# A new order for all queues of a pooled-attention and gated-convolution kernel, with ScalarE's one-column copy first

## The chip, the cores and the metric

The kernel runs on one core of a Trainium2 chip. A core has five engines, and the program gives each its own queue of instructions: TensorE (PE, with its weight loads shown apart as PEld), VectorE (DVE), ScalarE (ACT), GpSimd (POOL) and SyncE (SP). POOL and SP compute little here; they issue transfers. An engine waits on another only through semaphores. The metric is the device time of one execution in microseconds (us).

## The reference

The inputs are q, k and v, each 8 batches x 8 heads x 576 rows x 64 columns, and three weights. For each batch and head:

```
k_p, v_p = means of k and v over groups of 8 rows            # 576 -> 72 rows
attn     = softmax(q @ k_p.T / 8);  x = attn @ v_p           # heads side by side: 576 x 512
h        = relu(x @ w_in)                                    # 576 x 1024
conv     = w0 * h[row-1] + w1 * h[row] + w2 * h[row+1]       # per column of h, zero outside
out      = (h * sigmoid(conv)) @ w_out                       # 576 x 512
```

All inputs and the output are float32; the kernel computes in bf16 with float32 sums.

## The kernel before

**Attention of a batch.** k and v are added up over groups of 8 rows (three additions on DVE, or eight products with the identity on PE, `pmv`). PE transposes the sums of k (`kT`), and two copies spread them into `kz` (`kz.b.0`, `kz.b.1`). q is loaded by head and turned so that columns lie on partitions (`qT`, then the copies `qTe`); for batches 6 and 7 SP does that with transposing transfers (`qD`). A tile of scores is `sc` on PE and its exponential `exp` on ACT. Five tiles `av.b.t` per batch multiply with v; the reciprocal of the row sum and the scaling are `rc` and `nm` on DVE (lines 683 and 687). x is transposed by PE (`xt`, copied by `xte`), or from batch 3 on by SP (`xD`).

**The rest of a batch.** h comes in eight blocks of 128 columns, f = 0 to 7: `mm1.b.f` on PE and `relu.b.f` on ACT. The convolution goes by pairs of blocks, in one of three forms, which the table `alt` gives per pair ("c1.3" is the pair of blocks 2 and 3 in batch 1): form 0 works off PE, with two products by a tap (`cp0`, `cp2`, either on ACT, line 769, or on DVE, line 771), two additions on DVE (`ca0`, `ca2`, lines 776 and 781) and the sigmoid on ACT as a tanh (line 788); form 2 does both blocks on PE, with three diagonal weights per block (`dw`, line 407 on ACT or 409 on DVE, made once at the start for each block number that any pair needs) and the tanh straight from PE's result (line 805); form 1 does the first block off PE and the second on PE. Then DVE computes the gate (`tg1`, line 832) and the product (`g`, line 838). Two batches are a pair; its 9 tiles of 128 output rows are `mm2` on PE (line 863) with eight products each, a copy `oe` (ACT, line 888, or DVE) and a store.

**Batch 0** is treated apart so that work can start early: k comes in float32 through SP, q in two loads, of 64 and of 32 partitions (`ldq0.0` and `ldq0.1`, line 250). Scores, exponentials and `mm1` of batch 0 are split the same way, x = 0 for the larger part. Until data arrive, PE multiplies zeros (`fill`, line 231).

**What sets the order.** All work is first written down as 1,077 operations with their dependences. The table `order` is one list of these operations' numbers; every engine's queue is that list with the other engines' operations left out. An entry such as 77@B0 also gives the operation its PSUM buffer (three of kind A, two of kind B), and 106A0/77 puts 106 blocks of fill, of 128 columns each, ahead of it. The table `act` names the operations that may run on either engine and shall run on ACT; the rest of those run on DVE. So nothing of the order is decided at run time, and an instruction that waits holds up all that stands behind it on its engine.

**ScalarE's first operation.** `aw` copies one column of a small tile `wrm` (line 341); no other operation reads its result. ScalarE needs its function table loaded once, and the built program places that load ahead of ScalarE's first computing instruction, whichever that is.

Of the kernel before, what the change touches and what calls it, by code (L numbers as in the profile page):

```python
# [16 lines left out]
        "15 52 0 41 4 47 18 53 49 19 48 61 50 60 57 3 59 5 16 73 56 54 74 58 55 75 76 65 106A0/77@B0 6@B1 84@A0 7 36 21 78 86 17 85 62 42 "  # L17
        "17A1/80@B1 44 40 64 82@A1 81 63 79 87 83 139 88 35A2/98@B0 94@B1 43 106@A0 99 89 102@A1 140 100@A2 95 110@B0 90 103 112@B1 91 34 "
        "111 92 107 93 29 101 114@A0 23 39 108@B0 119@A1 113 115 109 124@A2 116 25 104@B1 96@B0 125 105 117@A0 97 126 118 120 13B1/129@A2 "
        "20 121 127@B0 134@A0 27 128 130 122@B1 33 156@A1 131 32 123 154@B0 135 152@A2 136 35 203@B1 155 204 8 132@A0 31 9 223@B0 28 205 51 "  # L20
        "157 133 137@B1 69 224 10 138 158 146 198@A0 153 199 201@B1 70 22 147 218@A1 200 226@A2 11 67 148 225 219 68 1 14 202 206@A0 24 227 "
        "13 149@B0 220 208 221@B1 210 150 252@A1 12 66 231 222 151 207 254@B1 26 229 253 169@A0 45 165@A2 37 209 240@B0 170 30 228 242@A1 "
        "166 232 163@A0 71 72 243 238@A2 211 164 212 143 256@A1 239 213 241 167@A0 255 244@A2 257 283 258@B0 245 171@A1 215 284 248@A2 172 "
        "285 277 259 144 46 230 286@B1 168 233 291@B0 249 289@A1 38 293@A0 214 290 246@A2 294 234 260@A1 216 235 287 217 262@A0 288 247 292 "
        "159@B1 263 250 236 261 301@A0 251 280 309@A2 160 302 141 161 307@A1 162 310 237 3B0/173@A0 281 308 305@A2 145 174 264 306 "
        "3B0/178@A1 175 3B0/183@A2 265 188@A0 142 176@B0 179 276 184 266@B1 295 180 177 401 189 185 400 190 186@B0 267 181@A1 191@A0 193@A2 "
        "187 268@B1 194 278 279 195 282 296 303@A2 192 269 271@B0 297 182 298 304 299 300 407 196@B1 272 311@A0 316@A1 197 408 321@A2 317 "
        "273@B0 409 312 322 520 318 323 521 326@A1 313 274 410@B1 419 413@A2 327 411 328 417@B0 415@A0 412 418 361@A1 416 539 375@A0 362 "
        "527 336@A1 376 528 414 351@A0 529 337 329@B0 352 431@A1 433@A2 420 432 319@B1 434 429@A0 341 349@A1 330 320 421 430 427@A2 422 "
        "314@B0 350 424 525 331@A0 366 428 324@B1 340 403 373@A1 332 405 333 406 425@A2 423 374 359@A0 342 402 325 343 355@A1 364 426 650 "  # L30
        "360 435@A2 643 530@B1 356 353@A0 531 315 363 532 338@A1 436 437 354 440@A2 339 438@B0 441 334@B1 357 344 444@A0 442 345@A1 522 439 "
        "367 537@A2 335 346 535@B0 538 533@B1 536 471@A1 380 534 365 379 445 549@A2 377 472 368 660@B0 550 656@B1 446 658@A1 369 553@A2 347 "
        "447 483@A0 659 657 378 554 651 485@A1 443 484 348 370 652 545@A0 498@A2 661 765 546 381 2 644 486 458@A0 524 382 499 404 448@A1 "
        "371 459 551@A2 523 372 653@B0 552 662 456@A0 449 384 358 496@A2 383 450 457 451 385 469@A1 654 386 655 452@A0 476 470 387@B1 453 "
        "487 454 540 497 455 461 547@A0 460 672@A1 541 270 673 670@A2 503 390@B0 542 671 462 649 543 548 647 463 473 771 645 668@A0 492@A1 "
        "669 544 646 772 555@A2 388 526 488 559@A0 493 556 489 392@B1 648 464 560 490 502 778 557 589@A1 777 558 561 474 563@A2 500 605@A0 "
        "780 773 393 501 590 564 774@B1 565 606 465@A1 779 504 775 676@A0 475 477 591@A2 466 275 505 562 391 478 567@A1 677 395@B0 568 491 "
        "467 566 569 592 663 479 389 571@A0 570 468 577@A1 776 480 572 573 674@A2 578 397@B1 664 574 506 494 665 675 495 768 507 789@A0 770 "
        "481 787@A1 616@A2 790 767 508 595 788 769 593 575@A0 781 617 782 596 603@A1 666 764 509 576 766 791@A2 667 604 618@A0 482 594 607 "
        "581 700@A1 792 580 609 597 742@A2 701 579 398 582 714@A1 583 743 619 783 698@A2 584 715 608 598 678@A0 682@A1 699 679 510@B1 623 "  # L40
        "784 396 786 585 683 680 684 620 686@A2 681 612@A0 687 586 688 712@A1 685 719 587 717 613 793@A2 621 512@B0 610 689 794 588 622 892 "
        "394 713 624 690@A0 611 795@A2 691 785 728@A1 625 796 511 886 694@A2 600 515@B1 614 692 729 705 695 887 693 696 627 726@A0 615 599 "
        "697 797@A1 716 516 740@A2 718 702 626 399 601 517@B1 798 727 703 706 733 799 704 847@A0 602 800 513 628 831@A1 848 629 514 518 "
        "801@A0 707 741 630@B0 519 730 709 802 888 708 803 720 805@A2 832 809@A0 732 806 889@B1 731 817@A1 807 890 631 893 861@A2 810 818 "
        "710 895 734 744 845@A1 746 735 894 633@B0 745 811 711 862 804 846 748 833@A0 634 721 808 891 813@A1 737 823 635@B0 896 834 747 736 "
        "837 897 722 903@A0 814 836 907@A2 638@B1 835 636 749 723 815 908 724 816 751 819@A1 738 839 904 901@A2 812 820 725 640@B0 824 821 "
        "739 632 750 637 898 905@A0 822 859@A1 849 906 825 902 909@A0 838 860 826 931@A2 851 827 866 933@A1 840 932 900 910 899 947@A2 752 "
        "934 852 828 753 911@A0 959@A1 641 865 864 948 829 754@B0 850 841 912 913 863 853 914 639 915@A0 867 945@A2 960 842 854 919@A1 935 "
        "756@B1 936 920 921 855 916 922 917 946 973@A1 856 830 642 757 937 923@A0 868 927@A2 755 759@B1 952 924 928 929 869 857 930 938 950 "
        "961@A2 925 870 843 758 975@A0 760 918 844 962 871 761@B0 976 858 926 949 872 963 939 873@B1 762 940 974 966 941 964 876@B0 980 965 "  # L50
        "967 942 874 951 1025@A0 875 978 968 763 977 1013@A1 943 970 953 1011@A2 981 1014 1026 954 1039@A1 1012 944 969 1027@A0 1016 1018 "
        "955 979 878@B1 1015 956 982 877 1017 971 1028 1019 997@A2 879 957 984 881@B0 972 983 1020 998 1029 1021 1032 999@A0 985 1003 958 "
        "883@B1 1030 986 882 1031 1033 1022 987@B0 1034 1000 884 1002 1001 1036 885 1023 989@B1 880 1004 1040 1005 1035 1006 988 1041@A0 "
        "1037 990 1038 1008 991 992@B0 1024 1007 1042 1009 1043 1010 994@B1 1045 1044 1046 993 1047 1053@A0 995 1048 996 1050 1057@B0 1049 "
        "1051 1061@B1 1052 1054 1058 1055 1062 1059 1056 1065@A0 1063 1060 1064 1066 1069@B0 1071 1070@B1 1067 1072 1068 1073 1075 1074 "
# [917 lines left out]
```

## Time and profile before

| what | value |
|---|---|
| time, median of 3 runs | 197.21 us (196.5 to 199.03) |
| profiled execution: its own time | 197.41 us |
| profiled execution: its span | 194.8 us |
| PE busy / idle in the span | 186.7 / 8.1 us |
| DVE busy | 165.9 us |
| ACT busy | 165.2 us |
| bytes read / written in HBM | 32.52 / 9.44 MB |

The span runs from the first to the last recorded instruction; the time of the same execution has 2.6 us more around it. Busy times are sums over the span, so they hide stages with different limits; matmuls overlap in the records, so a busy PE is not PE at its peak. "Idle before" an instruction is named with what ended it.

### The profile page before, as it was taken

The page shows a single profiled execution, that of the slowest core. Times are in us where ns is not written, and L with a number is a line of the kernel's source. Part 1 is how long each engine was busy: PE and PEld are TensorE (multiplying, and loading weights), DVE is VectorE, ACT ScalarE, POOL GpSimd, SP SyncE. Part 2 cuts the span into 40 slices and gives each one's busy share as a digit, 9 for nine tenths or more (in the row PEclk, how much of TensorE's full clock was granted, in tenths as well). Part 3 has the DMA queues.
Part 4 walks back from the last instruction along what each step waited for, and adds up shares of the span by engine and source line. Part 5 has one row for each costly group of instructions (what it writes and reads, how often), then busy time and mean ns, then how long its engine had stood idle before and what let it go on. Part 6 is the DMA issues. An engine that isn't in the chain of part 4 may idle for free.

```text
span 194.8 us, 4531 instructions
## 1 busy us (share of the span) xinstructions
PE 186.7 (96%) x1741; PEld 125.4 (64%) x1758; DVE 165.9 (85%) x391; ACT 165.2 (85%) x299; POOL 45.7 (23%) x85
## 2 busy tenths in 40 slices
PE   7887999999999999999999999999999999999993
PEld 2364896775687887767667766676566656655442
DVE  3563989997968799999999999999999999999720
ACT  0079999974478999999999999999999999999832
POOL 8872066086323503351044000000000000000000
PEclk9999999999999999999999999999999999999999
DMA  5999999979999997899956994659241463005344
GB/s 144 248 158 184 206 195 183 207 89 194 190 205 203 193 205 113 101 207 147 252 129 87 202 153 145 227 171 131 40 161 30 135 175 151 16 0 223 145 155 177
DMA packets 40201, 30.58 MB, mean 157 GB/s; under 512 B 18012, under 2 KB 35124, under 8 KB 40180
## 3 DMA queue, kind: packets, MB, share of 16 engines
q0 software_dynamic: 17920, 15.67, 53.0%
q1 hardware_dynamic: 22260, 14.63, 27.4%
q8 instruction: 13, 0.21, 0.5%
q14 instruction: 8, 0.07, 0.1%
HBM read 32.52 MB, written 9.44 MB: 215 GB/s over the span
## 4 chain that ended last, share of the span: by engine, by line
PE 56%; DVE 20%; ACT 16%; DMA 3%; issue 2%; DVEq 0%
PE psfB L863 20%; PE psfA L747 16%; ACT tg L788 4%; DVE xx L687 3%; PE psfA L670 3%; DMA osb<-in_k_dram 3%; DVE cv L771 3%; DVE cv L776 3%; ACT attnT L652 3%; DVE gT L838 2%; DVE cv L781 2%; PE psfA L863 2%; PE psfA L644 2%; ACT hT L738 2%; PE psfA L800 2%
## 5 line engine op out<-in xcount | busy, mean ns | idle before, releaser
L863 PE MATMUL psfB<-w_out,gT 128*128 128x512 bf16 (+1 forms) x266 | 62.1, 373 | 0.7
L747 PE MATMUL psfA<-xT,w_in 128*128 128x288 bf16 x448 | 60.6, 286 | 0.3 <-ACT hT L753 0.2
L747 PEld LDWEIGHTS <-w_in 128*128 128x128 bf16 x448 | 43.1, 98 | 14.3 <-issue 1.5
L863 PEld LDWEIGHTS <-gT 128*128 128x128 bf16 x296 | 28.5, 98 | 28.1 <-DVE gT L838 0.3
L788 ACT ACTIVATE tg<-cv,cs 128x576 bf16<-128x576 bf16 x54 | 40.9, 779 | 0.8 <-DVE cv L781 0.8
L753 ACT ACTIVATE hT<-psfA 128x576 bf16<-128x576 f32 x56 | 36.0, 658 | 2.9 <-PE psfA L747 2.6
L687 DVE TENSOR_TENSOR xx<-psfA,rr 128x512 bf16<-128x512 f32 x40 | 27.0, 684 | 0.6
L771 DVE TENSOR_SCALAR cv<-hT,cr 128x576 bf16<-128x576 bf16 x75 | 25.7, 367 | 1.1 <-ACT hT L738 0.8
L769 ACT ACTIVATE cv<-hT,cr 128x576 bf16<-128x576 bf16 x33 | 24.9, 776 | 0.1
L295 POOL DMA_DIRECT2D v_b<-in_v_dram x32 | 16.4, 517 | 36.5 <-DVE vs L533 22.9
L838 DVE TENSOR_TENSOR gT<-tg,hT 128x1152 bf16<-128x1152 bf16 x32 | 23.8, 753 | 0.2
L888 ACT COPY osb<-psfB 128x512 f32<-128x512 f32 x32 | 18.5, 588 | 5.5 <-PE psfB L863 5.5
L652 ACT ACTIVATE attnT<-psfA 128x576 bf16<-128x576 f32 x35 | 22.0, 658 | 0.1
L781 DVE TENSOR_TENSOR cv<-cv 128x1152 bf16<-128x1152 bf16 (+1 forms) x29 | 20.5, 713 | 0.5
L776 DVE TENSOR_TENSOR cv<-cv,hT 128x1152 bf16<-128x1152 bf16 (+1 forms) x29 | 20.2, 709 | 0.1
L670 PE MATMUL psfA<-vblk,attnT 128*128 128x130 bf16 x160 | 15.5, 220 | 1.3 <-ACT attnT L633 1.2
L832 DVE TENSOR_SCALAR tg<-tg 128x1152 bf16<-128x1152 bf16 x32 | 14.2, 450 | 2.6 <-ACT tg L788 2.3
L670 PEld LDWEIGHTS <-attnT 128*128 128x128 bf16 x160 | 11.9, 98 | 4.0 <-issue 1.1
L231 PE MATMUL pswA<-zero 128*128 128x512 bf16 (+1 forms) x42 | 10.9, 420 | 1.4 <-DVE zero L333 1.1
L683 DVE RECIPROCAL rr<-psfA 128x8 f32<-128x8 f32 x40 | 7.7, 199 | 4.8 <-PE psfA L674 4.8
L674 PE MATMUL psfA<-vblk,attnT 128*128 128x130 bf16 x80 | 11.2, 221 | 0.0
L644 PE MATMUL psfA<-qT,kz 128*128 128x288 bf16 x56 | 10.6, 286 | 0.0
(105 smaller groups left out, 221.2 us busy)
## 6 DMA issues: line engine op xcount, KB each, us to landing
out_dram<-osb SPq DMA_DIRECT2D x14, 512.0 KB, 3.0
q_b<-in_q_dram POOLq DMA_DIRECT2D x7, 576.0 KB, 8.1
k_b<-in_k_dram POOLq DMA_DIRECT2D x7, 512.0 KB, 9.5
v_b<-in_v_dram POOLq DMA_DIRECT2D x7, 512.0 KB, 8.6
out_dram<-osb SPq DMA_DIRECT2D x7, 256.0 KB, 2.1
osb<-in_k_dram SPq DMA_DIRECT2D x1, 1024.0 KB, 6.5
w_in<-in_moe_w_in_dram POOLq DMA_DIRECT2D x2, 512.0 KB, 10.9
w_out<-in_moe_w_out_dram POOLq DMA_DIRECT2D x2, 512.0 KB, 9.8
```

Source lines behind the costliest of these rows:

```text
L652: nc.scalar.activation(out=at(m)[:, t, :].rearrange("p (r i j) -> p r i j", i=2, j=3), in_=slot(key)[:, :, 0:HC].rearrange("p i (j r) -> p ...
L670: nc.tensor.matmul(out=a[:, g, c * w:(c + 2) * w], lhsT=attnT[m][:, S * s + u0:S * s + u0 + P], rhs=vblk[m][:, 2 * s:2 * s + 2, :].rearran ...
L687: nc.vector.tensor_tensor(out=xx[i3].rearrange("p (g h e) -> p g h e", g=2, h=4), in0=av_view()[:, :, :, 0:D], in1=rr[i3].rearrange("p (g ...
L747: nc.tensor.matmul(out=t[:, i, 0:HC], lhsT=w_in[:, c, f * P:(f + 1) * P], rhs=xT[m][:, c, i * HC:(i + 1) * HC], start=(c == 0), stop=(c == ...
L753: nc.scalar.activation(out=hT[m][:, f, 2:S + 2].rearrange("p (i x) -> p i x", i=2), in_=slot(key)[:, :, 0:HC], func=ACT.Relu)
L769: nc.scalar.activation(out=cv[y][:, kk // 2, z, :], in_=src, func=ACT.Copy, scale=sc)
L771: nc.vector.tensor_scalar(out=cv[y][:, kk // 2, z, :], in0=src, scalar1=sc, scalar2=None, op0=OP.mult)
L776: nc.vector.tensor_tensor(out=cv[y][:, 0, 0:n, :], in0=cv[y][:, 0, 0:n, :], in1=H4[:, f:f + n, 2:S + 2], op=OP.add)
L781: nc.vector.tensor_tensor(out=cv[y][:, 0, 0:n, :], in0=cv[y][:, 0, 0:n, :], in1=cv[y][:, 1, 0:n, :], op=OP.add)
L788: nc.scalar.activation(out=tg[i3][:, z, :], in_=cv[y][:, 0, z, :], func=ACT.Tanh if half else ACT.Sigmoid, scale=cs[:, f + z:f + z + 1] if ...
L838: nc.vector.tensor_tensor(out=o_, in0=tg[i3], in1=hT[b % 2][:, f:f + 2, 2:S + 2], op=OP.mult)
L863: nc.tensor.matmul(out=a[:, 0, 0:j1 - j0], lhsT=g[:, c, t * P:(t + 1) * P], rhs=w_out[:, c, j0:j1], start=(c == 0), stop=(c == n_fb - 1))
```

## The change

Only tables change; the code is the same. In `alt` one entry differs, the pair of blocks 2 and 3 of batch 1 goes from form 2 to form 1. No other pair uses block 2 on PE, so its three diagonal weights are no longer made. `order` and `act` are replaced. Fill shrinks from 180 blocks to 139; the first 106 stay.

```diff
-        "15 52 0 41 4 47 18 53 49 19 48 61 50 60 57 3 59 5 16 73 56 54 74 58 55 75 76 65 106A0/77@B0 6@B1 84@A0 7 36 21 78 86 17 85 62 42 "
...
+        "43 49 0 3 1 4 46 44 15 50 47 2 57 5 38 18 58 19 16 55 17 70 54 53 56 71 51 72 52 73 45 106A0/74@B0 6@B1 75 7 2A0/79@A0 39 83 76 8 "
...
-        "dw6.1 qTe.0.1.0 qTe.0.0.0 kz.0.1 qTe.0.0.1 dw5.2 dw2.0 dw7.1 dw2.2 xte.0.0 dw1.0 xte.0.2 dw5.0 xte.0.1 dw6.0 qTeP.1.1 dw4.2 "
...
+        "kz.0.0 kz.0.1 qTe.0.0.1 qTe.0.0.0 qTe.0.1.0 dw5.0 dw5.2 dw7.0 dw6.0 qTeP.1.1 dw7.1 dw7.2 qTeP.1.2 xte.0.1 xte.0.2 dw3.2 xte.0.3 "
...
-    "alt": {"q1": 1, "v1": 1, "c0.5": 2, "c0.7": 2, "q2": 1, "c1.1": 1, "c1.3": 2, "q3": 1, "x3.1": 1, "x3.2": 1, "x3.3": 1, "x3.4": 1, "c2.1": 1, "c2.5": 1, "q4": 1, "x4.0": 1, "x4.1": 1, "x4.2": 1, "x4.3": 1, "x4.4": 1, "c3.5": 1, "q5": 1, "x5.0": 1, "x5.1": 1, "x5.2": 1, "x5.3": 1, "x5.4": 1, "q6": 2, "x6.0": 1, "x6.1": 1, "x6.2": 1, "x6.3": 1, "x6.4": 1, "q7": 2, "x7.0": 1, "x7.1": 1, "x7.2": 1, "x7.3": 1, "x7.4": 1},
+    "alt": {"q1": 1, "v1": 1, "c0.5": 2, "c0.7": 2, "q2": 1, "c1.1": 1, "c1.3": 1, "q3": 1, "x3.1": 1, "x3.2": 1, "x3.3": 1, "x3.4": 1, "c2.1": 1, "c2.5": 1, "q4": 1, "x4.0": 1, "x4.1": 1, "x4.2": 1, "x4.3": 1, "x4.4": 1, "c3.5": 1, "q5": 1, "x5.0": 1, "x5.1": 1, "x5.2": 1, "x5.3": 1, "x5.4": 1, "q6": 2, "x6.0": 1, "x6.1": 1, "x6.2": 1, "x6.3": 1, "x6.4": 1, "q7": 2, "x7.0": 1, "x7.1": 1, "x7.2": 1, "x7.3": 1, "x7.4": 1},
```

In sums per engine: PE loses the 6 matmuls of one block's convolution. ACT gets two more tap products, one more output copy (`oe.2.4`) and one more q copy, gives up two `dw`, and has one tanh of form 0 in place of one from PE's result. DVE gets two additions for one block (half the size of a pair's), and gives up one `dw`, one output copy and one q copy; its count of tap products stays at 75.

At the head of ScalarE's queue stood the following before (dw is a diagonal weight, qT the turned q, kz the spread sums of k, attnT the exponentials, all of batch 0):

```order
L407 ACT_TABLE_LOAD
L407 ACTIVATE dw_117<-ident,cw 128x128
L573 COPY qT_87<-psbA 128x24x32
L573 COPY qT_87<-psbB 128x12x64
L507 COPY kz_85<-psbB 64x4x72
L573 COPY qT_87<-psbA 128x12x64
L633 ACTIVATE attnT_89<-psfB 128x384 x2
```

With the change the same queue begins so:

```order
L341 ACT_TABLE_LOAD
L341 COPY wrm<-wrm 128x1
L507 COPY kz_85<-psbB 64x4x72 x2
L573 COPY qT_87<-psbA 128x12x64
L573 COPY qT_87<-psbB 128x12x64
L573 COPY qT_87<-psbB 128x24x32
L633 ACTIVATE attnT_89<-psfB 128x384
```

The table load now belongs to the one-column copy, which waits only for a small memset that DVE does second; before, it belonged to a diagonal weight, which waits for the convolution's taps. Both halves of kz are now copied by ACT (DVE did one), and the larger part of q is copied first.

At the head of GpSimd's queue stood, after its constants (q_b0 takes the 64 and the 32 partitions of q, v_b0 the two halves of v and four tails of 16 partitions, all of batch 0; q_b1 and k_b1 are of batch 1):

```order
L394 MEMSET mask_65 128x780
L398 ISA
L398 AFFINE_SELECT mask_65<-mask_65 128x260 x2
L250 DMA q_b0_78<-in_q_dram 32x8x384
L250 DMA q_b0_78<-in_q_dram 64x8x384
...
L290 DMA v_b0_76<-in_v_dram 128x2x512
L282 DMA k_b1_75<-in_k_dram 64x512
L255 DMA q_b1_79<-in_q_dram 96x8x384
L398 AFFINE_SELECT mask_65<-mask_65 128x4x65
L303 DMA w_in_66<-in_moe_w_in_dram 128x4x512
```

With the change, from the same place:

```order
L394 MEMSET mask_65 128x780
L250 DMA q_b0_78<-in_q_dram 64x8x384
L398 AFFINE_SELECT mask_65<-mask_65 128x260
L250 DMA q_b0_78<-in_q_dram 32x8x384
L398 AFFINE_SELECT mask_65<-mask_65 128x260
L398 AFFINE_SELECT mask_65<-mask_65 128x4x65
L295 DMA v_b0_76<-in_v_dram 16x512
L398 AFFINE_SELECT mask_65<-mask_65 128x4x65
L295 DMA v_b0_76<-in_v_dram 16x512 x3
L290 DMA v_b0_76<-in_v_dram 128x2x512 x2
L255 DMA q_b1_79<-in_q_dram 96x8x384
L303 DMA w_in_66<-in_moe_w_in_dram 128x4x512
```

The 64-partition part of q is now the first load, the mask and all four tails stand ahead of both halves of v, and one short load of batch 1 no longer stands ahead of its q and of the first half of w_in. Not shown: three memsets and the identity now stand ahead of the mask.

Further on in the same queue (v_b0 is v of batch 2, k_b0 is k of batch 4, k_b1 k of batch 3; the 16-partition loads into v_b1 are tails of batch 3's v, which overwrite those of batch 1):

```order
L295 DMA v_b1_77<-in_v_dram 16x512
L290 DMA v_b0_76<-in_v_dram 128x4x512
L295 DMA v_b1_77<-in_v_dram 16x512
L295 DMA v_b0_76<-in_v_dram 16x512 x2
L278 DMA k_b1_75<-in_k_dram 128x4x512
```

This is what stands there with the change:

```order
L290 DMA v_b0_76<-in_v_dram 128x4x512
L282 DMA k_b1_75<-in_k_dram 64x512
L295 DMA v_b1_77<-in_v_dram 16x512 x2
L282 DMA k_b0_74<-in_k_dram 64x512
L278 DMA k_b0_74<-in_k_dram 128x4x512
L278 DMA k_b1_75<-in_k_dram 128x4x512
```

The load of batch 2's v moved ahead of the first tail of batch 3, and the load of batch 4's k ahead of that of batch 3's k.

90 rows, old and new, of the table PARAMS are left out of this document.

## Prediction

> **What bounds the kernel now.** I read the page's totals and chain first, then the busy time by stage, then the chain in order of time, and last the start by the timeline.
>
> ```profile
> span 194.8 us, 4531 instructions
> PE 56%; DVE 20%; ACT 16%; DMA 3%; issue 2%; DVEq 0%
> ```
>
> The chain of waits lies on PE for over half the span, but DVE and ACT own a third. The stages show why (columns: the stretch in us, its length, then busy us and instructions of PE, weight loads, DVE, ACT, POOL, then granted clock, DMA share, GB/s):
>
> ```profile
> 0.00:20.00 20.00, 16.61 (x183) 9.07 (x187) 9.63 (x29) 8.64 (x21) 12.88 (x29) 1.00 1.02 184
> 20.00:40.00 20.00, 19.57 (x276) 15.37 (x275) 18.26 (x53) 19.43 (x46) 7.25 (x15) 1.00 1.22 194
> 40.00:60.00 20.00, 19.77 (x229) 14.09 (x228) 16.47 (x40) 12.05 (x23) 10.02 (x16) 1.00 1.12 174
> 60.00:180.00 120.00, 119.12 (x1001) 81.05 (x1011) 116.55 (x265) 117.26 (x200) 15.52 (x26) 1.00 0.70 143
> ```
>
> From 60 to 180 us three engines are full at once: of 120 us PE idles 0.9, DVE 3.4, ACT 2.7. There an order can hardly save anything, and each new wait shows. Idle time of size stands in the first 20 us, and between 40 and 60 on ACT (8.0 us), where PE is the bound. Pieces of the chain (start, us, what) show who ends which stretch:
>
> ```profile
> 64.49 0.74 PE psfA L800 x6
> 101.13 0.65 DVE cv L771 x2
> 137.64 0.65 ACT attnT L652
> 144.93 1.14 PE psfA L747 x8
> ```
>
> The chain is on PE to about 91 us (one block's convolution, 0.74 us, lies on it), on ACT to 101, on DVE to 137, on ACT to 145, and then on PE to the end.
>
> **The start.** These are rows of the timeline (start, us, engine, line, instruction):
>
> ```profile
> 9.95 0.45 PE L501 MATMUL psbB<-ident,ksum 128*128 128x128 bf16 x5 [0.75 <-DVE ksum L482]
> 10.88 1.28 ACT L407 ACT_TABLE_LOAD   x1 [10.88 <-DVE cw L361]
> 12.17 0.40 ACT L407 ACTIVATE dw<-ident,cw 128x128 bf16<-128x128 bf16 x1
> 12.48 0.78 ACT L573 COPY qT<-psbA 128x768 bf16<-128x768 bf16 x1
> 13.99 0.39 ACT L507 COPY kz<-psbB 64x288 bf16<-64x288 bf16 x1
> 14.40 0.80 ACT L573 COPY qT<-psbA 128x768 bf16<-128x768 bf16 x1
> 15.61 0.87 ACT L633 ACTIVATE attnT<-psfB 128x384 bf16<-128x384 f32 x2 [0.41 <-PE psfB L625]
> 17.97 0.40 PE L670 MATMUL psfA<-vblk,attnT 128*128 128x130 bf16 x4 [1.16 <-ACT attnT L633]
> 18.52 0.21 DVE L683 RECIPROCAL rr<-psfA 128x8 f32<-128x8 f32 x1 [3.11 <-PE psfA L674]
> 22.86 0.83 PE L732 MATMUL psfB<-xT,w_in 128*128 128x128 bf16 x8
> ```
>
> ACT waits 10.88 us for the taps, spends 1.28 on the table load and 0.3 on the diagonal weight, and only then empties PE's buffers; the exponentials, the first `av` and all of DVE's scaling (idle 3.11) hang on that. With the change the load lies in ACT's idle time. After `kT` (9.95 + 0.45) come two kz copies of 0.39 and three q copies of 0.80: the first exponential starts at 10.4 + 0.8 + 2.4 = 13.6 in place of 15.61, and its score tile is computed under the last q copy. Ahead of the first `av` stand five wide exponentials (0.87 for two, so 0.44 each) and two narrow ones (0.35, the last row of the groups below): 13.6 + 2.9 = 16.5 in place of 17.97, a lead of **1.5 us**.
>
> Two loads must not undo it (GpSimd's queue; under the DMA rows, the last number is us from issue to landing):
>
> ```profile
> q_b<-in_q_dram POOLq DMA_DIRECT2D x1, 384.0 KB, 7.4
> v_b<-in_v_dram POOLq DMA_DIRECT2D x1, 256.0 KB, 5.6
> w_in<-in_moe_w_in_dram POOLq DMA_DIRECT2D x1, 512.0 KB, 9.1
> 7.54 0.75 POOL L290 DMA_DIRECT2D v_b<-in_v_dram  x1
> 10.84 0.80 POOL L255 DMA_DIRECT2D q_b<-in_q_dram  x1 [1.41 <-DMA q_b<-in_q_dram]
> 12.02 0.77 POOL L303 DMA_DIRECT2D w_in<-in_moe_w_in_dram  x1
> 13.26 0.56 DVE L521 TENSOR_TENSOR v_b<-v_b 128x768 bf16<-128x768 bf16 x1
> 14.95 0.29 DVE L550 TENSOR_TENSOR vblk<-vs,mask 128x256 bf16<-128x256 bf16 x1
> ```
>
> The 64-row part of q takes 7.4 us; issued at about 2.5 now, it lands by 9.9, ahead of `kT`. The 32-row part follows the mask by some 1.2 us and is needed last. The second half of v is issued about 1 us later (three tails now stand ahead), so it lands at 7.54 + 1.0 + 5.6 = 14.1; from its landing at 13.1 to the end of the last v product at 15.24 the row before took 2.1, which gives 16.2: just inside the 16.5. POOL's load of batch 1's q waited 1.41 us for a landing of batch 0's q; that wait comes earlier, and with one load less between, w_in is issued about 1 us before 12.02 and lands by some 20.1 in place of 21.1. DVE's queue then has 1.2 us of small work more between its scalings, but only 0.6 of it ahead of the tile for the first `mm1`; four reciprocals with scaling at 0.84 (18.52 to 19.37 is one) and a transposition give 17.05 + 4.0 + 0.2 = 21.3 in place of 22.86, again 1.5. Bounds: nothing, if a load is late by that much, and 2.0, the whole lead of the exponentials.
>
> **The rest of the sum.** These groups (busy us, mean ns) price the moved work:
>
> ```profile
> L800 PE MATMUL psfA<-hT,dw 128*128 128x288 bf16 x60 | 8.8, 286 | 0.0
> L788 ACT ACTIVATE tg<-cv,cs 128x576 bf16<-128x576 bf16 x54 | 40.9, 779 | 0.8 <-DVE cv L781 0.8
> L769 ACT ACTIVATE cv<-hT,cr 128x576 bf16<-128x576 bf16 x33 | 24.9, 776 | 0.1
> L805 ACT ACTIVATE tg<-psfA 128x576 bf16<-128x576 f32 x10 | 6.4, 659 | 0.1
> L888 ACT COPY osb<-psfB 128x512 f32<-128x512 f32 x32 | 18.5, 588 | 5.5 <-PE psfB L863 5.5
> L594 ACT COPY qT<-psbA 128x768 bf16<-128x768 bf16 x4 | 3.2, 811 | 0.0
> L407 ACT ACTIVATE dw<-ident,cw 128x128 bf16<-128x128 bf16 x11 | 4.5, 419 | 0.0
> L776 DVE TENSOR_TENSOR cv<-cv,hT 128x576 bf16<-128x576 bf16 x4 | 1.7, 437 | 0.0
> L633 ACT ACTIVATE attnT<-psfB 128x192 bf16<-128x192 f32 x4 | 1.1, 348 | 0.0
> ```
>
> From 20 to 40 us ACT is all but full (19.43 of 20). It has one diagonal weight less there (-0.42) and one tap product more (+0.78): +0.36. PE saves six matmuls of one convolution, **-0.74** by the chain's piece, in a stretch that PE ends; the rivals below say when that is worth nothing. The fill taken away costs and gains nothing in the sum, since the fill that went stood in waits.
>
> In the full stage ACT gets one more tap product (0.78), the output copy (0.59), the q copy (0.81) and the dearer tanh (0.779 - 0.659 = 0.12): **+2.3** against 2.7 of idle. DVE gets two half additions (0.44 each) and one tap product that went the other way at the start (0.37), and gives up the output copy (0.7 by ACT's row, the nearest) and the q copy (0.5, from the start of one 0.80 copy less DVE's faster reading, an estimate): about nothing. What ACT's extra costs is not in the trace. Below is nothing, if it all falls into ACT's idle time; above is 2.3, if none does. The chain lies on ACT for 9 + 8 of these 120 us, which is near the lower end, yet nearly all of ACT's idle would have to be used, which the order before does not do. I take a third, +0.8.
>
> The sum on the profiled execution's own 197.41 (span 194.8 and 2.6 around it): -1.5 + 0.36 - 0.74 + 0.8 = -1.1, so **196.3**. That execution was 0.2 above the median of 197.21, within the three runs' 196.5 to 199.03.
>
> By the Trainium skill's ScalarE: Activation LUTs, What ACT_TABLE_LOAD costs, a load of about 1.28 us is followed by a drain of about 1.38 us. The row of the load agrees on 1.28, but the next activation begins at 12.17, 0.01 after its end, so no drain shows here. By the page the start would gain 1.4 more and the sum would be 194.9.
>
> **The rivals.**
>
> *ScalarE takes over the bound (slower than before).* If ACT keeps its 2.7 us of waits in the full stage because its queue waits in order, its 2.3 of added work lengthens the stage in full, and PE's 0.74 is then worth nothing: 197.41 - 1.5 + 0.36 + 2.3 = 198.6, and more with every new wait. It decides once ACT uses less than 1.2 us of that idle time, which would bring back 197.4. For it: 117.26 of 120 busy. Against it: an ACT queue of more even work (tap products by batch 2 to 7 go from 5, 5, 8, 2, 8, 4 to 6, 6, 6, 6, 5, 5) where the chain was on DVE, which loses none of its slack.
>
> *The middle gains too.* Between 40 and 60 POOL's queue was held:
>
> ```profile
> 39.75 0.49 POOL L295 DMA_DIRECT2D v_b<-in_v_dram  x1 [5.31 <-PE psfA L644]
> ```
>
> That tail held batch 2's v, which now stands ahead of it. If batches 2 to 4 then start without waits, the stretch around 40 to 43, where PE did single `av` tiles between fill, gives 1.0, the start its full 2.0, and ACT's extra is hidden: 197.41 - 2.0 - 0.74 - 1.0 = 193.7. Against it: PE is the bound from 43 on, and batch 3's k now lands behind batch 4's.
>
> *The clock of PE.* The weight loads of the first fill show a clock that had to rise:
>
> ```profile
> 5.30 0.15 PEld L231 LDWEIGHTS <-zero 128*128 128x128 bf16 x1 [0.28 <-issue]
> 5.66 3.37 PEld L231 LDWEIGHTS <-zero 128*128 128x128 bf16 x16 [0.21 <-issue]
> ```
>
> Up to 5.30 one matmul took 0.43 us (0.15 and 0.28), afterwards 0.21 (3.37 by 16), though the granted clock reads 1.00 in every stage. The change takes 42 of 52 blocks of fill out of 11 to 16 us, where PE then has some 2 us of work. If it slows down again for as long as at the start (5.66 - 1.06 = 4.6 us), it loses 2.3 us: 198.6. Against it: 1.16 us without work at 17 did nothing. The Trainium skill's TensorE: Matmul & The Clock Gate, What's actually happening, has PE fall to half its clock after an idle window of about 3.4 us and rise after as long a busy one; the trace agrees with the rise, and no wait in it is long enough to show the fall. By that rule pieces of work between the waits could keep it up.
>
> *The start doesn't lead.* q or v lands over 1 us later than reckoned, and what is left of the lead is eaten by ACT: 197.41 + 0.36 - 0.74 + 0.8 - 0.3 = 197.5.
>
> **How the numbers follow.** The forecast, 195 to 197.3: 0.46. ScalarE takes over, 197.6 to 201.5: 0.24. The middle gains, 192.8 to 194.8: 0.16. The clock: 0.07. No lead: 0.07. Two per cent (193.3 to 201.2) is about what a measurement of this kernel tells from no change. Faster by more takes half of the middle's cases and a little else, 0.10; slower by more takes the upper end of ScalarE's and the clock's cases, 0.09; the rest, 0.81. The range cuts off the lowest of the middle's cases and the highest of ScalarE's: 193.0 to 200.2.
>
> **What would show it.** ACT's table load before 3 us; the first exponential near 13.6, the first `av` near 16.5, the first `mm1` near 21.3. ACT's idle time from 60 to 180 below 2 us for the forecast, 2.7 or more for the first rival. Batch 2's v issued before 35. PE's matmuls of 128x130 and 128x288 at their 220 and 286 ns throughout, or longer for the clock. I am wrong altogether if new waits on PE of over 2 us appear after 60 us, whose cause would be an order that no row of before can show.

## The result and the profile after

Over 20 executions each, the changed kernel took 195.85 us in the median (193.7 to 201.5) and the kernel before 196.8 (195.53 to 200.44). The ratio, in which executions more than 1.5% above the fastest of their kernel are left out, is **0.9908**, with a 95% interval of 0.9884 to 0.9933: a little faster, and within 2%. In a second comparison the same kernel stood at 196.25 against 196.87, a ratio of 0.9959 (0.9919 to 0.9999).

The profiled execution took 195.92 us, with a span of 194.2. From the page of the changed kernel: the granted clock in 40 slices, and the chain by engine.

```profile
PEclk9985999999999999999999999999999999999999
PE 84%; ACT 13%; issue 1%; DVE 0%; ACTq 0%
```

The span is 0.6 shorter than before. The chain now lies on PE for 84% (56 before) and hardly on DVE. And the third and fourth slices show what no slice of before did: TensorE's clock fell. The busy time by stage, in the same columns as before:

```profile
0.00:20.00 20.00, 18.06 (x201) 10.66 (x203) 10.48 (x33) 9.52 (x22) 12.97 (x32) 0.83 1.01 185
20.00:40.00 20.00, 19.50 (x251) 15.08 (x252) 17.53 (x47) 19.40 (x46) 8.94 (x15) 1.00 1.15 179
40.00:60.00 20.00, 19.56 (x224) 13.66 (x224) 16.87 (x41) 12.18 (x22) 8.28 (x13) 1.00 1.17 186
60.00:180.00 120.00, 119.20 (x995) 80.73 (x1007) 117.85 (x265) 118.55 (x202) 15.40 (x26) 1.00 0.71 143
```

From 60 to 180 us all three engines are fuller than before. ACT's idle time there is 1.45 us (2.7 before): it took 1.3 us more work into the same 120 us. In the first 20 us the clock is 0.83 in the mean; the same view in steps of 2 us:

```profile
12.00:14.00 2.00, 1.62 (x15) 0.98 (x14) 0.95 (x4) 1.52 (x4) 2.00 (x4) 0.76 1.20 169
14.00:16.00 2.00, 1.88 (x7) 0.56 (x5) 1.90 (x7) 1.98 (x6) 1.22 (x5) 0.50 1.23 174
16.00:18.00 2.00, 1.73 (x17) 1.79 (x18) 1.02 (x5) 2.00 (x8) 0.05 (x1) 0.50 1.20 187
18.00:20.00 2.00, 1.94 (x38) 1.72 (x37) 1.56 (x5) 0.59 (x2) 0.00 (x0) 0.54 1.24 203
```

Half clock for 0.96 + 2 + 2 + 1.84 = 6.8 us, from about 13.0 to 19.8. The start itself, in rows of the timeline of the changed kernel (start, us, engine, line, instruction):

```profile
0.80 1.28 ACT L341 ACT_TABLE_LOAD   x1 [0.80 <-PEq L957]
9.34 0.44 PE L501 MATMUL psbB<-ident,ksum 128*128 128x128 bf16 x5
9.82 0.80 ACT L507 COPY kz<-psbB 64x288 bf16<-64x288 bf16 x2 [7.53 <-PE psbB L501]
12.91 0.52 ACT L633 ACTIVATE attnT<-psfB 128x384 bf16<-128x384 f32 x1
16.27 0.59 PE L670 MATMUL psfA<-vblk,attnT 128*128 128x130 bf16 x4 [0.29 <-ACT attnT L633]
18.55 1.46 PE L587 MATMUL psbB<-ident,q_b 96*64 96x96 bf16 x32
22.73 1.05 PE L732 MATMUL psfB<-xT,w_in 128*128 128x128 bf16 x12
```

The first exponential comes 2.7 us earlier than before, the first `av` 1.7, the first `mm1` only 0.13: the lead is lost between 16 and 22 us. (`kT` itself began 0.6 earlier, at 9.34 in place of 9.95, so that much of each lead is not ScalarE's.) The chain in order of time says where:

```profile
18.55 0.86 PE psbB L587 x16
19.43 0.80 ACT qT L594
20.82 0.69 ACT qT L594
21.52 0.59 ACT xT L705
22.89 0.88 PE psfB L732 x12
```

L587 and L594 turn and copy q of **batch 1**. In the new order two of these turnings stand ahead of `av.0.3` on PE (18.55), and two of the copies ahead of batch 0's x on ACT; before, all of batch 1's q stood behind the last `av` of batch 0, with its turnings still ahead of the first `mm1` and its copies behind those of the x that this `mm1` reads.

The rest of the gain lies outside the span. The time around it was 2.6 us in the profiled execution of before and is 1.7 here. That row of before was unusual: its median is 1.85 to 2.03 in three sets of executions, against 1.7 to 1.75 for the new order, so some 0.2 us of the medians is there.

### The profile page after: what moved, and what is told of

It is laid out like the page before. It is cut to its first block, busy times and chain, and to the rows that moved or that the text cites. A ratio compares the mean times of both kernels' runs of the same rounds, so it can differ in the third digit from the quotient of the medians.

```text
span 194.2 us, 4491 instructions
## 1 busy us (share of the span) xinstructions
PE 187.3 (96%) x1722; PEld 125.7 (65%) x1738; DVE 166.8 (86%) x390; ACT 166.9 (86%) x301; POOL 45.6 (23%) x85
## 4 chain that ended last, share of the span: by engine, by line
PE 84%; ACT 13%; issue 1%; DVE 0%; ACTq 0%
PE psfB L863 30%; PE psfA L747 28%; PE psfA L670 5%; PE pswA L231 5%; PE psfA L644 2%; PE psfA L674 2%; ACT attnT L652 2%; PE psfA L863 2%; PE psfA L800 2%; ACT tg L805 2%; ACT qT L594 1%; PE psfB L732 1%; ACT tg L788 1%; PE psbB L587 1%; PE psfA L732 1%; ACT attnT L633 1%
## 5 line engine op out<-in xcount | busy, mean ns | idle before, releaser
L863 PE MATMUL psfB<-w_out,gT 128*128 128x512 bf16 (+1 forms) x260 | 61.0, 376 | 0.6
L747 PEld LDWEIGHTS <-w_in 128*128 128x128 bf16 x448 | 42.9, 98 | 12.9 <-DVE xx L687 0.5
L788 ACT ACTIVATE tg<-cv,cs 128x576 bf16<-128x576 bf16 x55 | 42.5, 805 | 0.6 <-DVE cv L781 0.6
L753 ACT ACTIVATE hT<-psfA 128x576 bf16<-128x576 f32 x56 | 36.5, 669 | 1.9 <-PE psfA L747 1.5
L771 DVE TENSOR_SCALAR cv<-hT,cr 128x576 bf16<-128x576 bf16 x75 | 26.4, 369 | 1.1 <-ACT hT L738 0.6
L769 ACT ACTIVATE cv<-hT,cr 128x576 bf16<-128x576 bf16 x35 | 27.2, 806 | 0.1
L888 ACT COPY osb<-psfB 128x512 f32<-128x512 f32 x33 | 19.9, 615 | 2.4 <-PE psfB L863 1.1
L776 DVE TENSOR_TENSOR cv<-cv,hT 128x1152 bf16<-128x1152 bf16 (+1 forms) x30 | 21.0, 701 | 0.6 <-ACT cv L769 0.2
L670 PE MATMUL psfA<-vblk,attnT 128*128 128x130 bf16 x160 | 16.4, 227 | 0.9 <-ACT attnT L652 0.3
L674 PE MATMUL psfA<-vblk,attnT 128*128 128x130 bf16 x80 | 11.6, 228 | 0.0
L507 ACT COPY kz<-psbB 64x288 bf16<-64x288 bf16 x11 | 4.3, 391 | 7.8 <-PE psbB L501 7.7
L231 PE MATMUL pswA<-zero 128*128 128x512 bf16 (+1 forms) x34 | 9.6, 441 | 1.1 <-DVE wrm L337 1.1
```

Source lines behind the costliest of these rows:

```text
L670: nc.tensor.matmul(out=a[:, g, c * w:(c + 2) * w], lhsT=attnT[m][:, S * s + u0:S * s + u0 + P], rhs=vblk[m][:, 2 * s:2 * s + 2, :].rearran ...
L747: nc.tensor.matmul(out=t[:, i, 0:HC], lhsT=w_in[:, c, f * P:(f + 1) * P], rhs=xT[m][:, c, i * HC:(i + 1) * HC], start=(c == 0), stop=(c == ...
L753: nc.scalar.activation(out=hT[m][:, f, 2:S + 2].rearrange("p (i x) -> p i x", i=2), in_=slot(key)[:, :, 0:HC], func=ACT.Relu)
L769: nc.scalar.activation(out=cv[y][:, kk // 2, z, :], in_=src, func=ACT.Copy, scale=sc)
L771: nc.vector.tensor_scalar(out=cv[y][:, kk // 2, z, :], in0=src, scalar1=sc, scalar2=None, op0=OP.mult)
L776: nc.vector.tensor_tensor(out=cv[y][:, 0, 0:n, :], in0=cv[y][:, 0, 0:n, :], in1=H4[:, f:f + n, 2:S + 2], op=OP.add)
```

## The experiments

In the tables, a number with a letter (77@B0) is an operation with its PSUM buffer, and 35A2/ is fill ahead of it. The numbers in brackets behind a median are lowest and highest.

**Fill kept (e1).** The changed kernel, with 28 more blocks of fill between its first operations on PE: 38 up to the first `av`s, where the changed kernel has 10.

```diff
-... 81@B0 ... 4A1/107@B1 ... 4A1/109@B0 ... 91@A0 ... 95@A1 ... 111@A0
+... 4A2/81@B0 ... 8A1/107@B1 ... 6A1/109@B0 ... 6A2/91@A0 ... 6A2/95@A1 ... 6B0/111@A0
```

> The changed kernel, with 36 blocks of fill in the waits of the start where it has 10: 2 ahead of the first q transposes as in the change, 4 ahead of the last ones, 8, 6, 6 and 6 ahead of four score tiles, 6 ahead of the first av. Theory A (the clock): the changed kernel loses 6.8 us of full clock at the start in some executions, because the fill that covered 10 to 16 us is gone. Of its 20 runs, the 8 with a mean granted clock of 1.00 took 194.6 us on average and the 12 with 0.97 to 0.99 took 197.4. With the fill back every execution shows 1.00 and takes about 194.6, a ratio of 0.989 to the kernel before, and the spread of 7.8 us is gone. Theory B (the falling clock only goes with a slow execution and isn't its cause, since PE has idle time there): clocks of 0.98 may vanish, but the times stay near 195.9 with their spread. Theory C (fill has nothing to do with it): clocks of 0.98 stay.

195.54 us (194.97 to 200.93), ratio 0.9892 (0.9846 to 0.9939) to before: not to be told from the changed kernel. (The expectation says 36 blocks of fill; the list has 38.) Of the six executions four kept the clock, at 194.97 to 195.6 us, and two did not, so theory A fails, which has every execution at full clock and 194.6; B, much the same times and spread, comes nearest. Rows of its profile:

```profile
PEclk9999999999999999999999999999999999999999
18.32 0.87 PE L587 MATMUL psbB<-ident,q_b 96*64 96x96 bf16 x32 [0.67 <-DMA q_b<-in_q_dram]
21.02 0.38 PE L701 MATMUL psbB<-ident,xx 128*128 128x128 bf16 x4 [0.36 <-ACT qT L594]
22.08 1.05 PE L732 MATMUL psfB<-xT,w_in 128*128 128x128 bf16 x12
```

The clock stayed full, and the two turnings took 0.87 us in place of 1.46. Yet the first `mm1` came 13.2 us after `kT` (13.4 in the changed kernel, 12.9 before): PE now waited 0.67 for batch 1's q to land, and 0.36 for a copy of it on ACT ahead of the third transposition of batch 0's x. The fill has its own price too: the first `av` came 7.5 us after `kT`, in the changed kernel 6.9, before 8.0. So the fallen clock cost this profiled start some 0.2 us, or 0.3 against the changed kernel's second profile (e8, full clock, 13.1 us). With either clock the lead is gone by the first `mm1`; that the place of batch 1's q takes it is how I read these waits.

**The one-column copy alone (e2).** The kernel before, with `aw` and its memset moved to the heads of the queues.

```diff
-15 52 0 41 4 47 ... 68 1 14 ... 381 2 644 ...
+15 52 0 1 2 41 4 47 ... 68 14 ... 381 644 ...
```

> The kernel before, with only the small memset and ScalarE's one-column copy moved to the heads of their queues, so that the table load runs at about 1 us. Theory A (the start carries to the end): 1.28 us leave ScalarE's queue ahead of its first q copy, the first exponential moves from 15.6 to about 14.3, and the time falls by up to 1.3, to about 195.5 where the kernel before takes 196.8. Theory B (the start's lead is eaten before 60 us, by ScalarE and the order of PE's queue): the first exponential moves as much, the time stays at 196.8 within 0.4.

197.02 us (196.64 to 198.89), ratio 1.0000 (0.9973 to 1.0027). The copy that the title names gives nothing by itself, and the first half of both theories fails: the first exponential did not come 1.3 us earlier against `kT`. Rows of its timeline:

```profile
10.90 0.87 PE L231 MATMUL pswA<-zero 128*128 128x512 bf16 x4 [0.16 <-issue]
12.32 0.80 ACT L573 COPY qT<-psbB 128x768 bf16<-128x768 bf16 x1 [0.73 <-PE psbB L567]
12.81 1.86 PE L231 MATMUL pswA<-zero 128*128 128x512 bf16 x10 [0.16 <-issue]
14.87 0.87 ACT L633 ACTIVATE attnT<-psfB 128x384 bf16<-128x384 f32 x2 [0.52 <-PE psfB L625]
```

ACT is free early and then waits 0.73 and 0.52 us for PE, which works off 0.87 and 1.86 us of fill: the first exponential comes 5.6 us after `kT`, as before (5.7). The fill of the order before stood beside the table load, and was as long. The profile of before shows it, in a stretch of its chain that the prediction left out:

```profile
13.50 1.86 PE pswA L231 x10
15.36 0.23 PE psfB L625
15.61 1.25 ACT attnT L633 x3
```

The chain comes to the first exponentials through fill, and not through ScalarE's copies.

**The copy first, and that fill out (e9).**

```diff
...
-17A1/80@B1 ... 35A2/98@B0
+80@B1 ... 98@B0
```

> The kernel before with two edits: the one-column copy first, and the 17 blocks of fill ahead of q's turning and the 35 ahead of the scores left out. Theory (in the order before, PE's fill and not ScalarE's table load held the first scores): without the fill ScalarE's copies stand back to back, so the first exponential begins about 4.6 us after the start of kT instead of 5.6, the first av about 6.9 instead of 7.9, and the time falls by up to 1 us against before, unless the granted clock falls in the gap. Rival 1 (the loads of v or the copies hold the start, the fill stood in waits as I had reckoned): the first exponential stays within 0.2 us of 5.6 after kT. Rival 2 (the lead is lost again before the first mm1 of batch 0, whatever the start): first av 1 us earlier, but vb of batch 1 still ends about 30.6 us after kT, and the time equals that of before within 0.3%.

197.66 us (196.67 to 198.59), ratio 1.0027 (0.9998 to 1.0055). Rows of two views, by 2 us and of the timeline:

```profile
12.00:14.00 2.00, 0.14 (x1) 0.20 (x2) 1.86 (x7) 1.76 (x3) 2.00 (x3) 0.87 0.99 119
14.00:16.00 2.00, 2.00 (x13) 0.59 (x12) 1.26 (x5) 1.53 (x4) 1.54 (x6) 0.50 1.28 194
9.56 0.44 PE L501 MATMUL psbB<-ident,ksum 128*128 128x128 bf16 x5
14.38 0.87 ACT L633 ACTIVATE attnT<-psfB 128x384 bf16<-128x384 f32 x2 [0.56 <-PE psfB L625]
17.69 0.64 PE L670 MATMUL psfA<-vblk,attnT 128*128 128x130 bf16 x4
23.11 0.83 PE L732 MATMUL psfB<-xT,w_in 128*128 128x128 bf16 x8
```

The fill was on the path: the first exponential now comes 4.8 us after `kT`, 0.8 earlier than in e2 (the theory said 4.6). But without the fill PE idles 1.86 of 2 us at 12, the clock halves, the groups of `av` take 0.64 in place of 0.40, and the first `mm1` comes 13.6 us after `kT`, where e2 has it after 12.8. The mean granted clock was between 0.973 and 0.983 in all 12 executions. So, by these two profiles, the fill cost 0.8 us and held off a loss of 1.5.

**The two halves of the new order (e3, e4).** e3 has the changed order up to the first `mm1` and that of before from there on; e4 has the order of before to that point, then the changed one.

```diff
-"alt": { ... "c1.3": 2, ... }
+"alt": { ... "c1.3": 1, ... }
```

That line is e4's; e3 keeps form 2.

> The changed kernel's order up to the first mm1 of batch 0 (table load, q, masks, loads, less fill), and from there the order of the kernel before, with blocks 2 and 3 of batch 1 on PE as before. Theory A: this start is worth 1.5 us where the clock stays up and -1.2 or so where it falls, as in the changed kernel: a mean clock below 1.00 in part of the runs, those near 197.5, the others near 195.3. Theory B: the start's lead doesn't reach the end even at full clock: 196.8 at a clock of 1.00, and about 198 where it falls.

> The order of the kernel before up to the first mm1 of batch 0 (with its fill), and from there the changed kernel's order, with block 2 of batch 1 off PE. Theory A: PE's 0.74 less and ScalarE's 2.3 more about cancel: 196.8 within 0.5, clock 1.00 in each run. Theory B: the gain of the change lies in this part: about 195.4 or less, clock 1.00.

e3: 196.23 us (195.59 to 198.4), ratio 0.9966 (0.9931 to 1.0001). e4: 198.41 (197.63 to 207.88), ratio 1.0068 (1.0042 to 1.0094). The halves don't add: together they give 0.991 to 0.996, apart 0.997 and 1.007. e3 lies between its two theories: seven executions kept the clock and took 195.6 to 196.5 us, the other five 196.0 to 198.4. e4 misses both of its own, 196.8 and 195.4. As I read it, the rest was written for its own start. In e4, of PE's waits between 20 and 42 us (summed, times, longest),

```profile
PE psfB L732 <- ACT qT L594: 0.8, 1, 0.8
PE psfA L732 <- ACT xT L705: 0.4, 1, 0.4
```

and `vb.1.0` ends 1.4 us later than before (41.95 for 40.53). From there on e4 needs 151.8 us to the end of the last output copy, the changed kernel 151.0, before 151.6.

**Batch 1's q behind batch 0's `av` (e5).** e1, with the turnings of batch 1's q and two of their copies moved behind batch 0's first copy of x.

```diff
-... 1B0/151@B0 122 153@B1 123 152 126@A0 117 149@A2 ... 114@B0 154 ... 115 129@A0
+... 122 123 126@A0 117 ... 114@B0 ... 115 151@B0 153@B1 152 154 149@A2 129@A0
```

> The fill_kept kernel (changed order, 36 blocks of fill in the start), with batch 1's three q transposes and two of their copies moved behind the last av of batch 0 and the copy of its first x tile, so that av.0.3 no longer waits behind the landing of batch 1's q (0.67 us there in that kernel's profile, at 18.3). Theory A (the start carries): the first mm1 comes about 1.3 us earlier, 11.9 after kT in place of 13.2, and the time falls by as much, to about 194.0 where the kernel before takes 197.1. Theory B (the middle is bound by the transfers, the start's lead doesn't reach it): the first mm1 comes as much earlier, and the time stays within 0.4 of the fill_kept kernel's 195.3.

199.12 us (197.04 to 204.21), ratio 1.0047 (1.0002 to 1.0092): it made things worse. Rows of its profile:

```profile
18.48 0.40 PE L670 MATMUL psfA<-vblk,attnT 128*128 128x130 bf16 x4 [0.41 <-DVE rr L683]
20.07 0.40 PE L701 MATMUL psbA<-ident,xx 128*128 128x128 bf16 x4 [0.85 <-DVE xx L687]
21.14 0.40 PE L670 MATMUL psfA<-vblk,attnT 128*128 128x130 bf16 x4 [0.45 <-ACT xT L705]
21.59 0.87 PE L587 MATMUL psbB<-ident,q_b 96*64 96x96 bf16 x32
23.01 1.08 PE L732 MATMUL psfB<-xT,w_in 128*128 128x128 bf16 x12
```

PE waits 0.41, 0.85 and 0.45 us for DVE's scalings and ACT's copies instead, and the first `mm1` comes 13.6 us after `kT` (expected: 11.9). Batch 1's q had been lying in these waits. But the run neither cures the cause that I had named nor refutes it. The three turnings only moved to another place ahead of the first `mm1`: they begin at 21.59, when the copies of x that this `mm1` reads have just ended (21.58, which is 12.2 us after `kT`). And the 0.85 comes from the order itself, since PE's queue transposes x by tiles 0, 1, 2, while DVE scales them as 0, 2, 1. A start with batch 1's q behind the first `mm1` was not run.

**The convolution back on PE (e6).** The changed kernel with the pair c1.3 in form 2 again, its block put between the neighbours it had time for.

```diff
-"alt": { ... "c1.3": 1, ... }
+"alt": { ... "c1.3": 2, ... }
```

> The changed kernel with the one entry of the table put back: blocks 2 and 3 of batch 1 both on PE, the three diagonal weights of block 2 made again (two on ScalarE, one on VectorE), its tap products, two half additions and tanh left out. Prediction: PE's 0.74 more against ScalarE's 2.3 and a third: the changed kernel's time within 0.3. Theory A (PE is the bound there): 0.7 slower than the changed kernel in the same call. Theory B (ScalarE and VectorE are): up to 0.8 faster.

200.06 us (196.87 to 204.62); against the changed kernel on the same chip 1.0067 / 0.9959 = 1.011. The sign of the whole edit agrees with the term of -0.74, and its size, some 2 us, is more than that. The place that I gave the block may be part of it, and so may another thing, seen in its profiled execution, the longest of the 14: PE waited 4.15 us for a transposing transfer of x.

```profile
111.10 5.63 PE L748 MATMUL psfA<-xT,w_in 128*128 128x288 bf16 x31 [4.15 <-DMA xT<-xx]
```

(The lines of this kernel are numbered one higher.) So the edit as a whole costs time, and what the form alone is worth stays open, its sign included.

**Batch 2's v early (e7).** The kernel before, with the load of batch 2's v ahead of the first tail of batch 3's.

```diff
-... 251 280 309@A2 160 302 141 161 ...
+... 251 141 280 309@A2 160 302 161 ...
```

> The kernel before with one load moved in GpSimd's queue: batch 2's v ahead of the tail of batch 3's v that waits 5.3 us for PE. Its place in the queue frees the transfer engines' pause around 39 to 42 us. Theory B (transfers bound the middle): batch 3's k lands 1 to 2 us before the 49.2 of the kernel before, batch 3's v before 58.8, VectorE's sums of batch 3's k follow, and the time falls by about 1, to 196.1 where the kernel before takes 197.1. Theory A (PE bounds the middle): the landings come earlier, the time stays within 0.3.

197.81 us (196.28 to 200.39), ratio 1.0016 (0.9973 to 1.0058): moving that load alone gains nothing. Its profiled execution shows something else, a fall of the clock at the start of the old order:

```profile
15.10 3.33 PE L231 MATMUL pswA<-zero 128*128 128x512 bf16 x11
```

The fill ahead of the scores took 3.33 us (1.86 in e2), and everything behind it came late: `vb.1.0` ended 3.05 us later than in the profile of before, and the last output copy 3.04. Here a delay of the start was carried to the end in full.

**The changed kernel again (e8).**

> The changed kernel itself, beside the others on the same chip: 0.990 of the kernel before, as in its 20 runs, in two groups, near 195.0 and near 197.5, if the theory of the clock holds; one group if not.

The time is given above. The two groups that the theory of the clock asks for do not show: the four executions at full clock took 196.1 to 197.3 us, five of the six at 0.989 to 0.991 took 195.1 to 196.5, and the other three 197.6 to 204.9. In its profile the clock stayed full and the first `mm1` came at 22.02, 0.7 earlier than in the first profile, but the span was 1.3 longer:

```profile
105.57 3.96 PE L747 MATMUL psfA<-xT,w_in 128*128 128x288 bf16 x31 [1.28 <-DMA xT<-xx]
```

At this place, batch 4's first `mm1`, the last transposing transfer landed 0.7 us ahead in the first profile of the changed kernel, 1.0 in that of before, and here 1.28 too late.

**More time for that transfer, and less fill (e10, e11).** e10 is e1 with the last output tile of the first pair moved to just ahead of batch 4's `mm1`; e11 has, besides, 92 blocks in the first fill in place of 106.

```diff
-... 789@A2 781 397@B1 790 ... 604 667 700@A0
+... 789@A2 781 790 ... 604 667 397@B1 700@A0
```

```diff
-... 106A0/74@B0 ...
+... 92A0/74@B0 ...
```

> The changed kernel with 36 blocks of fill in place of 10 at the start (as in e1), and one output tile of the first pair (its last) moved behind two blocks of mm1, so that PE has 1.9 us of other work just ahead of the first mm1 of batch 4. Theory (executions differ by when the transposing transfers of x land): PE's wait for xT stays below 0.2 us in the profile, no execution lies over 198.5 us, and the median falls to 195.0 or below. Rival (the spread comes from the clock or from elsewhere): executions at 198 to 201 us remain, and the median stays at e1's 195.5.

> The same kernel as e10, with 92 blocks of fill ahead of kT in place of 106. Theory (in the changed order kT waits for the end of the fill, since k lands early): kT begins about 0.6 us earlier against its fellow, near 8.5, right behind the sums of k, and the whole execution ends 0.4 to 0.6 us earlier if no later load takes it back. Rival 1 (k sets kT): nothing moves. Rival 2 (the later loads, batch 1's q and w_in, set the first 23 us): kT earlier, first mm1 at the same time, the same total.

e10: 197.35 us (196.89 to 201.64), ratio 1.0004 (0.9973 to 1.0034); e11: 200.28 (197.69 to 205.26), 1.0076 (1.0028 to 1.0124). Both theories fall. In e10 PE did not wait for the transfer, but two of its executions still took over 200 us, and even its shortest, 196.89, is longer than four of e1's six:

```profile
100.67 1.14 PE L747 MATMUL psfA<-xT,w_in 128*128 128x288 bf16 x8 [0.74 <-ACT attnT L652]
102.42 0.40 PE L644 MATMUL psfA<-qT,kz 128*128 128x288 bf16 x2 [0.60 <-ACT attnT L652]
103.64 1.89 PE L863 MATMUL psfB<-w_out,gT 128*128 128x512 bf16 x8
```

The tile had stood where PE has to let ACT finish its exponentials. With it gone PE waits 0.74 and 0.60 us there, and the last output copy ends 1.5 us later than in e1, 0.3 more of a lead at the start notwithstanding. In e11 `kT` starts at 9.13, in e10 at 9.21:

```profile
9.13 0.45 PE L501 MATMUL psbB<-ident,ksum 128*128 128x128 bf16 x5 [0.34 <-DVE ksum L482]
```

k's sums set it (the expectation's first rival), and with the shorter fill the clock fell in 8 of 12 executions, against 3 of 12 in e10.

## Why the prediction was right, and where it was not

The forecast was 196.3 us, the median is 195.85, within the range and the likeliest case's own range. The sum of the terms, -1.1, is close to what was measured, -0.95 between the medians and -1.5 between the profiled executions. But it is close because errors of opposite sign met in it: in the profiled executions the start gave 1.4 us less than forecast, and the rest and the time around the span some 1.8 more. That the total came out is luck. Term by term, from the two profiles:

| term | forecast | measured |
|---|---|---|
| start, up to the first `mm1` | -1.5 | -0.13 |
| from there to the end of `vb.1.0`, about 40 us | +0.36 | +0.07 |
| from there to the last output copy: PE -0.74, ACT +0.8 | +0.06 | -0.59 |
| around the span | 0 | -0.9 (about -0.2 typically) |

**The start.** Its first half came as worked out, and better: table load at 0.80 (said: before 3), first exponential at 12.91 (13.6), first `av` at 16.27 (16.5). What is better there is `kT`'s earlier begin, which the sum had not claimed: counted from `kT`, the first exponential came after 3.57 us (3.65), and the first `av` after 6.93 (6.55), later than worked out. The loads came as reckoned too; from the rows of the DMA issues, the 64-row part of q went out at 2.18 and took 7.5, so it landed at 9.7 (9.9), and POOL's wait for batch 0's q came at 9.96 in place of 10.84:

```profile
2.18 0.83 POOL L250 DMA_DIRECT2D q_b<-in_q_dram  x1
q_b<-in_q_dram POOLq DMA_DIRECT2D x1, 384.0 KB, 7.5
9.96 0.80 POOL L255 DMA_DIRECT2D q_b<-in_q_dram  x1 [1.43 <-DMA q_b<-in_q_dram]
```

The step that failed is "four reciprocals with scaling at 0.84 (18.52 to 19.37 is one) and a transposition give 17.05 + 4.0 + 0.2 = 21.3". It took DVE's queue for the bound and counted what moved on DVE's, ACT's and POOL's queues, but not what moved on PE's, the turning of batch 1's q ahead of `av.0.3`. First `mm1` 22.73. The third scaling of x, in the profile of before and then of the changed kernel:

```profile
20.44 0.69 DVE L687 TENSOR_TENSOR xx<-psfA,rr 128x512 bf16<-128x512 f32 x1
19.50 0.69 DVE L687 TENSOR_TENSOR xx<-psfA,rr 128x512 bf16<-128x512 f32 x1
```

It ended 0.94 us earlier, and the first `mm1`, which reads at most three tiles of x, came 1.7 us behind it before and 2.5 us behind it now (2.5 in e1 too, at full clock). In that time PE waits for no scaling; it and ACT work on batch 1's q and on the transposed x. So DVE was not the bound: that is shown. That batch 1's q is the whole reason is not, since e5 left it ahead of the first `mm1`. The same step also missed that the table load did not carry the old start: e2 shows that the fill beside it was as long. That fill is what the changed start left out (e9), and the text had put it down as standing "in waits", worth nothing.

**What the start still gave.** `kT` began 0.6 earlier in the profile of the changed kernel. Over the profiled executions it began on average at 9.6 with the old start (five kernels, 9.28 to 10.0) and 9.2 with the new (eight, 8.88 to 9.69). This lead of about 0.4 us does not come through ScalarE's queue, for which `kT` does not wait. k is brought in by SP, and its sums began at 6.0 to 6.5 us with the new start, at 6.2 to 7.3 with the old. That the tails of v went out later (4.73 and 5.62 in place of 3.88 and 4.95) is one difference, not tried by itself. It can't be all: e2 and e9 have the old tails and the early table load, and their sums began at 6.23 and 6.35, those of the three other old starts at 6.67 to 7.33. What moves them stays open.

**PE's 0.74 and ACT's 2.3.** The measured -0.59 lies 0.65 below the forecast. Over five profiles of each order the same stretch took 151.0 to 151.9 with the new rest (the changed kernel, e1, e4, e5, and e8 without its wait) and 151.5 to 152.8 with the old (the kernel before, e2, e3, e7, e9), means 151.5 and 152.0: -0.4. The two sets overlap, and with e8's wait left in the difference is 0.2, so the two terms can't be told apart. If PE's 0.74 came in full, ACT's extra work cost some 0.3 us, and the lower end was nearer than the third that I took. Of the 2.3 us that were added, ACT's busy time from 60 to 180 us shows 1.3. ACT's idle time fell to 1.45 us, below the 2 that was named for the forecast. *ScalarE takes over the bound* did not happen.

**The base.** The sum was made on 197.41, with 2.6 us around the span. With the usual 1.9 the base is 196.7 and the forecast 195.6, still within 0.3 of the median.

**The clock.** It was given 0.07, and it did fall. From `kT` to the first `av` PE showed no wait of more than 0.35 us, so what I named against it (1.16 us without work did nothing) was no evidence either way: it is not the longest gap that counts. The price was said to be 2.3 us. In the profiled execution it was 0.2 to 0.3 by the first `mm1` (against e1 and e8); in e1, at full clock, PE waited 0.67 us for a load there instead. In e7, where the fallen clock caught the long fill of the old start, it was 3.0, in one execution. As sign of it I had named matmuls that are longer throughout; the groups of the whole span show 227 ns for `av` in place of 220 and an unchanged 286 for `mm1`:

```profile
L747 PE MATMUL psfA<-xT,w_in 128*128 128x288 bf16 x448 | 60.8, 286 | 0.0
L670 PE MATMUL psfA<-vblk,attnT 128*128 128x130 bf16 x160 | 16.4, 227 | 0.9 <-ACT attnT L652 0.3
```

Over the whole span it hardly shows; by stage it does.

**The middle.** Batch 2's v was issued at 33.36, before 35 as named, but e7 shows no gain from this load by itself. *The start doesn't lead* is, in effect, the rival that came true for the first 22 us, for another reason than a late load.

## What to carry to other kernels

When a bound is taken away at the start, follow the new chain through every engine's queue up to the point where the lead is to be booked: here ScalarE's 10.9 us of waiting were replaced first by fill on TensorE, and then, by the chain, by another batch's work that now stood ahead. Fill that looks like idle padding has a price and a use, and each is to be read from its own rows: the place where it delays a result, and the granted clock by stage. In a schedule with three full engines a tile that looks free to move can be what covers another engine's work: look at what stood around it before moving it.

## What the runs showed of the hardware

**The clock falls in steps.** In the profile the half clock lasted 6.8 us, in e3's 3.4. The mean granted clocks of whole executions lie near 1.000, 0.991, 0.982 and 0.974, that is, steps of 0.0087, or 1.7 us of a span of 195: the loss of one stretch of 3.4 us at half clock. By the Trainium skill's TensorE: Matmul & The Clock Gate, What's actually happening, the activity is watched in free-running windows of 3413 ns, and the clock has only two values; these numbers agree.

**It falls without a long gap.** In the 3.4 us ahead of the fall, 9.6 to 13.0, PE was busy for 3.00 us by its records in the changed kernel, for 2.94 in e1 and 2.89 before, where it did not fall. The records of busy time do not tell the cases apart; these are mostly products of 32 and 64 columns. What goes with it over many executions is fill: those with a mean clock of at least 0.998 were 106 of 129 with the start of before (e2, e4, e7 and the kernel before), 23 of 58 with the changed start (the changed kernel, e3, e6), 20 of 30 with e1's fill (e1, e5, e10), 4 of 12 in e11 and none of 12 in e9. Where fill alone differs, e9 has none of 12 and e2 10 of 12, e11 4 of 12 and e10 9 of 12. The mean of an execution does not tell where the clock fell, though. In the first 20 executions of the changed kernel these took 194.6 us in the mean (8 of them, 193.7 to 195.22), the other 12 took 197.4. In e8, the same kernel, four executions with a lower clock, 195.05 to 195.54 us, were shorter than each of the four at full clock, 196.06 to 197.26. How much of the first difference is the clock's own loss, and how much comes with it, was not settled; e1, with more fill, was not clearly faster in the median.

**It falls behind a long gap too.** In e6 the clock read 0.50 from 112 to 114 us and 0.64 from 114 to 116, which is 3.4 us at half clock, right behind PE's wait of 4.15 us for a transfer. So a late transfer can bring a lower mean clock with it, beside its own wait.

**A transfer's landing is not fixed.** The wait for the same transposing transfers at the same place was 0, 1.28 and 4.15 us in three profiles (the changed kernel, e8 and e6) of kernels with one order of these transfers.
